# Attention with softmax normalised on GpSimd, every probability tile transposed by DMA, and V as the stationary operand

## The chip, the cores and the metric

The kernel runs on 1 core of one Trainium2 chip. Its time is the device time of one execution in microseconds (us). Before the change the median of three runs is 2014.84 us (2014.69 to 2027.13). A separate execution was profiled; its span, from the first to the last instruction, is 2008.4 us. The engines are PE (TensorE), DVE (VectorE), ACT (ScalarE), POOL (GpSimd) and SP (SyncE, which here only issues DMAs); PEld is the PE's weight load.

## What is computed

One transformer block with adaptive layer norm, on 2048 rows of width 640, batch 1:

```python
mod = silu(c) @ w_mod                       # six vectors of 640: sa, ca, ga, sb, cb, gb
h = layernorm(x) * (1 + ca) + sa
q = h @ wq                                  # 32 heads of 128; K and V come from a cache of 2048 rows
p = softmax(q @ k^T * 128**-0.5)            # 32 x 2048 x 2048
x = x + ga * ((p @ v) @ wo)
h = layernorm(x) * (1 + cb) + sb
u = gelu(layernorm(h) @ w1)                 # four column groups, shifted by +1, -1, +2, -2 rows
x1 = h + shifted(u) @ w2
x = x + gb * (x1 + gelu(layernorm(x1) @ w3) @ w4)   # width 1728 between w3 and w4
```

## The kernel before, in words

It is written by hand, engine by engine: each stage is a block with one instruction stream per engine, semaphores (`Ev`, `W`) order the streams, and a barrier ends the block.

**Head (L72-L176).** The six modulation vectors, then for 16 tiles of 128 rows layer norm on DVE, a transpose on PE and an evacuation on ACT into `hT`. Only when all 16 are done does the attention block begin.

**Attention (L179-L436).** 512 steps `s`: 32 heads of 16 query tiles of 128 rows. In a step PE multiplies a query tile with the 2048 keys (four matmuls of 512 columns into `Sps`, L327, two halves of 1024); DVE scales each half into `negS` and takes its minimum (L371); POOL takes the smaller of the two minima (L270); ACT makes the unnormalised exponentials `Pb` in bf16 (L399). Seven of eight tiles are transposed by a DMA from SP (L297), the eighth by PE (L312) with two copies by DVE (L363). Six steps later PE multiplies 16 transposed pieces as stationary operands with `Vaug` (V and a column of ones, 129 columns, L344), so that the row sum appears in column 128. DVE takes its reciprocal (L382), ACT scales the 128x128 result by it into `On` (L405), and POOL issues the DMA to DRAM (`o_scratch`, L285). For the next head PE transposes K and projects Q (`pe_job`, L228 and L233), ACT evacuates (L241, L244), and POOL issues all loads (L250-L256).

**Later stages.** Output projection with `wo`, residual and two layer norms per tile (L487, L525-L539), with `o_scratch` read back by DMA transposes (L471); a block for w1 and gelu (L585, L600); one for w2 and a layer norm (L618, L637); and one for w3, gelu, w4 and the end (L678-L714). Each begins with its own weight loads.

Of the kernel before, what the change touches and what calls it, by code (L numbers as in the profile page):

```python
# [8 lines left out]
F32 = mybir.dt.float32  # L9


class Ev:

    def __init__(self, nc, es, name):
        self.sem = es.enter_context(nc.semaphore(name))
        self.n = 0

    def inc(self, ins, k=1):
        ins.then_inc(self.sem, k)
        self.n += k  # L20
        return self.n


def W(eng, ev, val):
    if val > 0:
        eng.wait_ge(ev.sem, val)  # L26


def bass_adaLN_cond__mha_block_cached__mixer_s_mlp__prompt_kernel(
# [5 lines left out]
    assert DH == 128 and D % 128 == 0 and SQ % 512 == 0 and SK == 2048  # L35
# [5 lines left out]
    FL = FF - (NFT - 1) * 128  # L41
    G4 = D // 4
    SCALE = float(DH) ** -0.5
    EPS = 1e-5
    NG = H * NQT
    x2d = A_x[0]
    out2d = out[0]
    HD = D // 2
    NC2 = [(0, 512), (512, D - 512)]

    with ExitStack() as es:
        sb = lambda name, shape, dt: es.enter_context(nc.sbuf_tensor(name, shape, dt))
# [3 lines left out]
        mod_bc = sb("mod_bc", [128, 6 * D], F32)
        Sps = ps("Sps", [128, 2048], F32)
        PTp = ps("PTp", [128, 2048], BF16)
        Oaug = ps("Oaug", [128, 512], F32)
        QPp = ps("QPp", [128, 512], F32)  # L60
        QPb = QPp[:].bitcast(BF16)

        def ln_stats(v, src, st, mv, ev, ev2=None):
            v.bn_stats(st[:, 0:6], src[:, 0:HD])
            ev.inc(v.bn_stats(st[:, 6:12], src[:, HD:D]))
            W(v, ev, ev.n)
            (ev2 or ev).inc(v.bn_aggr(mv[:, 0:2], st[:, 0:12]))  # L67

        with ExitStack() as esA:
            sbA = lambda name, shape, dt: esA.enter_context(nc.sbuf_tensor(name, shape, dt))  # L70
            hT = sbA("hT", [128, KT, SQ], BF16)
            with ExitStack() as es0:  # L72
                sb0 = lambda name, shape, dt: es0.enter_context(nc.sbuf_tensor(name, shape, dt))
                c_sb = sb0("c_sb", [128, KT], BF16)
                c_f = sb0("c_f", [128, KT], F32)
                s_bc = sb0("s_bc", [128, KT, 128], BF16)
                ones_f = sb0("ones_f", [128, 128], F32)
                wmod = sb0("wmod", [128, KT, 6 * D], BF16)
                x_sb = sb0("x_sb", [128, NQT, D], BF16)
                st = sb0("st", [128, 2, 12], F32)  # L80
                mv = sb0("mv", [128, 2, 2], F32)
                sd = sb0("sd", [128, 2, 1], F32)
                rstd = sb0("rstd", [128, 2, 1], F32)
                xn = sb0("xn", [128, 2, D], F32)
                hA = sb0("hA", [128, 2, D], BF16)
                block = es0.enter_context(nc.Block())
                e_dc = Ev(nc, es0, "p_dc"); e_dw = Ev(nc, es0, "p_dw"); e_dx = Ev(nc, es0, "p_dx"); e_pool = Ev(nc, es0, "p_pool"); e_silu = Ev(nc, es0, "p_silu")
                e_sbc = Ev(nc, es0, "p_sbc"); e_mm = Ev(nc, es0, "p_mm"); e_mev = Ev(nc, es0, "p_mev")
                e_d = Ev(nc, es0, "p_d"); e_st = Ev(nc, es0, "p_st"); e_sq = Ev(nc, es0, "p_sq")
                e_hA = Ev(nc, es0, "p_hA"); e_tr = Ev(nc, es0, "p_tr"); e_hev = Ev(nc, es0, "p_hev")  # L90
                NCH = 8
                CW = 6 * D // NCH
                assert CW <= 512

                @block.sync
                def _(e):
                    with nc.allow_non_contiguous_dma(reason="tiny c vector"):
                        e_dc.inc(e.dma_start(c_sb[:], c[0].rearrange("(kt p) -> p kt", p=128)), 16)
                    e_dw.inc(e.dma_start(wmod[:], w_mod.rearrange("(kt p) n -> p kt n", p=128)), 16)
                    e_dx.inc(e.dma_start(x_sb[:], x2d.rearrange("(t p) d -> p t d", p=128)), 16)  # L100

                @block.gpsimd
                def _(g):
                    e_pool.inc(g.memset(ident[:], 0.0))
                    e_pool.inc(g.memset(ones_f[:], 1.0))
                    W(g, e_pool, 2)
                    e_pool.inc(g.affine_select(out=ident[:], in_=ident[:], pattern=[[-1, 128]],
                                               compare_op=ALU.not_equal, fill=1.0, base=0, channel_multiplier=1))

                @block.scalar  # L110
                def _(a):
                    W(a, e_dc, 16)
                    e_silu.inc(a.activation(c_f[:], c_sb[:], ACT.Silu))

                    def hev(qt):
                        b = qt % 2
                        W(a, e_tr, qt + 1)
                        e_hev.inc(a.copy(hT[:, :, qt * 128:(qt + 1) * 128],
                                         PTp[:, b * 1024:b * 1024 + KT * 128].rearrange("p (k q) -> p k q", k=KT)))
                    for qt in range(NQT):  # L120
                        b = qt % 2
                        W(a, e_st, qt + 1)
                        e_sq.inc(a.activation(sd[:, b], mv[:, b, 1:2], ACT.Sqrt, bias=float(EPS)))
                        if qt >= 1:
                            hev(qt - 1)
                    hev(NQT - 1)

                @block.tensor
                def _(t):
                    W(t, e_sbc, 1)  # L130
                    W(t, e_dw, 16)
                    for ch in range(NCH):
                        bank = Sps[:, (ch % 4) * 512:(ch % 4) * 512 + CW]
                        W(t, e_mev, ch - 3)
                        for kt in range(KT):
                            ins = t.matmul(bank, s_bc[:, kt, :], wmod[:, kt, ch * CW:(ch + 1) * CW],
                                           start=(kt == 0), stop=(kt == KT - 1))
                        e_mm.inc(ins)
                    W(t, e_pool, 3)
                    for qt in range(NQT):  # L140
                        b = qt % 2
                        W(t, e_hA, qt + 1)
                        W(t, e_hev, qt - 1)
                        for kt in range(KT):
                            ins = t.transpose(PTp[:, b * 1024 + kt * 128:b * 1024 + (kt + 1) * 128],
                                              hA[:, b, kt * 128:(kt + 1) * 128], ident[:])
                        e_tr.inc(ins)

                @block.vector
                def _(v):  # L150
                    W(v, e_silu, 1)
                    W(v, e_pool, 2)
                    for kt in range(KT):
                        ins = v.tensor_scalar(out=s_bc[:, kt, :], in0=ones_f[:], scalar1=c_f[:, kt:kt + 1],
                                              scalar2=None, op0=ALU.mult)
                    e_sbc.inc(ins)
                    for ch in range(NCH):
                        W(v, e_mm, ch + 1)
                        bank = Sps[:, (ch % 4) * 512:(ch % 4) * 512 + CW]
                        e_mev.inc(v.tensor_copy(mod_bc[:, ch * CW:(ch + 1) * CW], bank))  # L160
                    W(v, e_mev, NCH)
                    v.tensor_scalar_add(out=mod_bc[:, D:2 * D], in0=mod_bc[:, D:2 * D], scalar1=1.0)
                    e_d.inc(v.tensor_scalar_add(out=mod_bc[:, 4 * D:5 * D], in0=mod_bc[:, 4 * D:5 * D], scalar1=1.0))
                    W(v, e_d, e_d.n)
                    W(v, e_dx, 16)
                    for qt in range(NQT):
                        b = qt % 2
                        ln_stats(v, x_sb[:, qt, :], st[:, b], mv[:, b], e_d, e_st)
                        W(v, e_sq, qt + 1)
                        e_d.inc(v.reciprocal(rstd[:, b], sd[:, b]))  # L170
                        W(v, e_d, e_d.n)
                        e_d.inc(v.scalar_tensor_tensor(out=xn[:, b], in0=x_sb[:, qt, :], scalar=mv[:, b, 0:1],
                                                       in1=mod_bc[:, D:2 * D], op0=ALU.subtract, op1=ALU.mult))
# [5 lines left out]
            with ExitStack() as es1:  # L179
# [564 lines left out]
```

## Time and profile before

| what | us |
|---|---|
| median of three runs | 2014.84 |
| span of the profiled execution | 2008.4 |
| first attention op on DVE (L371) starts at | 104.1 |
| last one starts at | 1577.0 |
| first output-projection matmul (L487) starts at | 1624.8 |
| last one starts at | 1770.1 |
| PE, DVE, ACT, POOL busy | 1587.3, 1547.8, 1374.8, 662.8 |

The span falls into a head of 104 us, 512 attention steps in 1476 us, and 428 us behind them. Busy time is a union, and the PE's includes the latency of pipelined matmuls, so it doesn't say how near PE is to its peak. In the rows of the profile "x512 | 1025.2, 2003 | 213.9 <-POOL" reads: 512 instructions, busy 1025.2 us, 2003 ns one, and 213.9 us of idle time just before them that POOL ended most of. In a row of stretches stand the stretch and its length, busy time and count of PE, PEld, DVE, ACT and POOL, the granted PE clock (1.00 is full), the share of time in which DMA packets were under way (above 1 where packets overlap on an engine) and GB/s.

### The profile page before, as it was taken

What the parts mean: (1) busy time and instruction counts of PE and PEld (TensorE: products, weight loads), DVE (VectorE), ACT (ScalarE), POOL (GpSimd) and SP (SyncE); (2) the same over time, 40 slices, a digit from 0 to 9 for tenths busy, and PEclk for the clock granted to TensorE, in tenths of its full rate; (3) what the DMA queues carried; (4) which work ended last, traced back from release to release, by engine and by line L of the source; (5) the groups of instructions that cost most, each with busy time, mean ns of one, the idle gap of its engine ahead of it and who ended that gap; (6) DMA issues with size and microseconds to landing.
All of it is one profiled execution on the core that took longest, in us unless ns stands there. A gap on an engine that the chain in (4) does not pass through costs nothing. (4 is left out here: it accounts for less than half of the span.)

```text
span 2008.4 us, 39142 instructions
## 1 busy us (share of the span) xinstructions
PE 1587.3 (79%) x14480; PEld 993.0 (49%) x14708; DVE 1547.8 (77%) x3151; ACT 1374.8 (68%) x1428; POOL 662.8 (33%) x1321
## 2 busy tenths in 40 slices
PE   2388888888888888888888888888888469966798
PEld 1145555555555555555555555555555335533344
DVE  5588888898889888888888888888988437737025
ACT  1288888888888888888888888888888401143430
POOL 0224444444444444444444444444443200010000
PEclk7589999999999999999999999999999879989899
DMA  4189999999999989999988989999999775510201
GB/s 150 38 160 201 198 198 199 201 198 195 199 202 204 190 197 199 198 201 199 194 188 191 187 200 196 203 199 196 195 202 196 174 199 122 106 33 1 89 14 40
DMA packets 1044381, 333.95 MB, mean 166 GB/s; under 512 B 1011744, under 2 KB 1024992, under 8 KB 1044192
## 3 DMA queue, kind: packets, MB, share of 16 engines
q1 hardware_dynamic: 1013472, 275.81, 68.3%
q0 software_dynamic: 30720, 55.63, 10.6%
q8 instruction: 118, 1.93, 0.4%
q14 instruction: 71, 0.58, 0.1%
HBM read 60.26 MB, written 19.40 MB: 40 GB/s over the span
## 5 line engine op out<-in xcount | busy, mean ns | idle before, releaser
L371 DVE TENSOR_SCALAR_CACHE_REDUCE negS<-Sps 128x1024 f32<-128x1024 f32 x1024 | 1207.7, 1217 | 168.6 <-PE Sps L327 163.7
L399 ACT ACTIVATE Pb<-negS,nm 128x2048 bf16<-128x2048 f32 x512 | 1025.2, 2003 | 213.9 <-POOL nm L270 194.8
L327 PE MATMUL Sps<-KTs,QT 128*128 128x512 bf16 x1889 | 549.8, 387 | 162.7 <-DVE negS L371 142.2
L270 POOL TENSOR_SCALAR nm<-nm 128x1 f32<-128x1 f32 x512 | 145.3, 284 | 840.9 <-DVE negS L371 840.9
L327 PEld LDWEIGHTS Sps<-KTs,QT 128*128 128x128 bf16 x2048 | 154.3, 98 | 402.8 <-DVE negS L371 320.6
L344 PEld LDWEIGHTS PTp<-Vaug,PTs 128*128 128x128 bf16 x4096 | 263.0, 99 | 66.4 <-issue 24.0
L285 POOL DMA_DIRECT2D o_scratch<-On x512 | 289.3, 565 | 4.5 <-ACT On L405 4.0
L344 PEld LDWEIGHTS Oaug<-Vaug,PTs 128*128 128x128 bf16 x4096 | 259.6, 98 | 59.9 <-issue 1.1
L344 PE MATMUL PTp<-Vaug,PTs 128*128 128x129 bf16 x4096 | 286.9, 223 | 1.5 <-ACT On L405 1.2
L344 PE MATMUL Oaug<-Vaug,PTs 128*128 128x129 bf16 x4096 | 281.4, 220 | 0.0
L487 PE MATMUL Sps<-wo,OTj 128*128 128x128 bf16 (+1 forms) x1008 | 140.9, 301 | 38.6 <-DMA OTj<-o_scratch 37.8
L233 PE MATMUL QPp<-hT,wq 128*128 128x512 bf16 x607 | 155.9, 386 | 5.2 <-ACT QT L244 2.0
L487 PEld LDWEIGHTS Sps<-wo,OTj 128*128 128x128 bf16 x1024 | 80.1, 99 | 100.1 <-DMA OTj<-o_scratch 37.6
L435 ACT ACTIVATE sdB<-mvB 128x1 f32<-128x1 f32 x48 | 9.7, 203 | 158.3 <-DVE mvB L67 158.3
L312 PE MATMUL PTp<-ident,Pb 128*128 128x128 bf16 x1024 | 78.7, 220 | 43.3 <-ACT Pb L399 43.3
L256 POOL DMA_DIRECT2D Vaug<-in_A_v_cache_dram x128 | 104.9, 820 | 5.6 <-issue 5.5
L363 DVE COPY PTs<-PTp 128x1024 bf16<-128x1024 bf16 x128 | 86.8, 678 | 25.4 <-PE PTp L312 25.3
L250 POOL DMA_DIRECT2D Knat<-in_A_k_cache_dram x128 | 104.7, 820 | 0.4 <-issue 0.4
L709 DVE TENSOR_TENSOR t<-Sps,xb 128x640 f32<-128x640 f32 x16 | 13.2, 825 | 103.6 <-PE Sps L690 103.6
L405 ACT ACTIVATE On<-Oaug,rl 128x128 bf16<-128x128 f32 x256 | 89.7, 350 | 2.5 <-DVE rl L382 2.5
L405 ACT ACTIVATE On<-PTp,rl 128x128 bf16<-128x128 f32 x256 | 89.5, 350 | 2.0 <-DVE rl L382 2.0
L312 PEld LDWEIGHTS PTp<-ident,Pb 128*128 128x128 bf16 x1024 | 60.1, 98 | 54.6 <-ACT Pb L399 54.5
(72 smaller groups left out, 1127.6 us busy)
## 6 DMA issues: line engine op xcount, KB each, us to landing
Knat<-in_A_k_cache_dram POOLq DMA_DIRECT2D x128, 128.0 KB, 3.7
Vaug<-in_A_v_cache_dram POOLq DMA_DIRECT2D x128, 128.0 KB, 3.8
o_scratch<-On POOLq DMA_DIRECT2D x512, 32.0 KB, 3.3
PTs<-Pb SPq DMA_TRANSPOSE x448, 4.8
wq<-in_A_wq_dram POOLq DMA_DIRECT2D x32, 160.0 KB, 4.7
wo<-in_A_wo_dram SPq DMA_DIRECT2D x1, 5120.0 KB, 17.0
wmod<-in_w_mod_dram SPq DMA_DIRECT2D x1, 4800.0 KB, 14.8
x_sb<-in_A_x_dram SPq DMA_DIRECT2D x1, 2560.0 KB, 21.3
```

Of the source, the lines that this page charges most:

```text
L233: ins = t.matmul(QPp[:, 0:512], wq[:, hb, kk, :], hT[:, kk, cc * 512:(cc + 1) * 512], start=(kk == 0), stop=(kk == KT - 1))
L250: e_k[hb][pc // 2].inc(e.dma_start(Knat[:, hb, pc * 4:(pc + 1) * 4, :], A_k_cache[0, h, pc * 512:(pc + 1) * 512, :].rearrange("(t p) d -> ...
L256: e_v[hb].inc(e.dma_start(Vaug[:, hb, q * 4:(q + 1) * 4, 0:128], A_v_cache[0, h, q * 512:(q + 1) * 512, :].rearrange("(t p) d -> p t d", p ...
L270: e_nm.inc(g.tensor_scalar(out=nm[:, r8:r8 + 1], in0=nm0[:, r8:r8 + 1], scalar1=nm1[:, r8:r8 + 1], scalar2=None, op0=ALU.min))
L285: e_od[g_ % 8].inc(g.dma_start(o_scr[jj, :, hh, :], On[:, g_ % 8, :]), 16)
L312: ins = t.transpose(PTp[:, q * 128:(q + 1) * 128], Pb[:, b4, kt * 128:(kt + 1) * 128], ident[:])
L327: ins = t.matmul(Sps[:, col:col + 512], QT[:, hb, j * 128:(j + 1) * 128], KTs[:, hb, col:col + 512], start=True, stop=True)
L344: ins = t.matmul(ob[:, 0:129], PTs[:, b4, kt, :], Vaug[:, hb, kt, 0:129], start=(kt == 0), stop=(kt == NKT - 1))
L371: ins = v.tensor_scalar(out=negS[:, b, half * 1024:(half + 1) * 1024], in0=Sps[:, half * 1024:(half + 1) * 1024], scalar1=-SCALE, scalar2= ...
L399: e_exp.inc(a.activation(Pb[:, b4, :], negS[:, b, :], ACT.Exp, bias=nm[:, r8:r8 + 1], scale=-1.0))
L405: e_nrm.inc(a.activation(On[:, r8, :], OB[g_ % NOB][:, 0:128], ACT.Copy, scale=rl[:, r8:r8 + 1]))
L487: ins = t.matmul(YB[b][:, c0:c0 + cw], OTj[:, jj % 3, hh, :], wo[:, hh, c0:c0 + cw], start=(hh == 0), stop=(hh == H - 1))
```

## The change

Semaphores by hand are replaced by a list of operations (`Program.op`) with the tokens that each reads and writes: waits follow from the tokens, each engine runs its operations in the order in which they are written, and a DMA on SP waits in SP's queue for its inputs. An operation waits by a semaphore also for what its own engine wrote before it, where it reads that.

In the attention K arrives by DMA transpose (`ld_kt`). DVE's second half takes the first half's minimum as a per-row scalar, so no POOL operation joins them. ACT writes the exponentials in float32 (`E_`, 3 buffers) and their row sum by its accumulator; DVE takes its reciprocal two steps later; POOL multiplies the tile of 128x2048 by it into bf16 (`Pn`, 3 buffers); SP transposes every tile by DMA. Four tiles make a chunk (`PTs`, 3 chunks). V's pieces are stationary, 512 transposed columns stream, and 16 matmuls give O^T for four tiles. They are issued four to a step, two behind each half's score matmuls, and begin 8 steps behind the chunk's first tile (`PVL = 8`). ACT evacuates the chunk, and SP stores it transposed into `o_scratch`.

```diff
-                            ins = v.tensor_scalar(
-                                out=negS[:, b, half * 1024:(half + 1) * 1024],
...
-                        e_exp.inc(a.activation(Pb[:, b4, :], negS[:, b, :], ACT.Exp, bias=nm[:, r8:r8 + 1], scale=-1.0))
...
+                op("vector", lambda v: v.tensor_scalar(out=o_, in0=i_, scalar1=-SCALE, scalar2=nm0[:, r8:r8 + 1], op0=ALU.mult,
+                                                       op1=ALU.min, accum_out=nm[:, r8:r8 + 1]),
...
+            op("scalar", lambda a: a.activation(E_[:, be, :], negS[:, b, :], ACT.Exp, bias=nm[:, r8:r8 + 1], scale=-1.0,
+                                                accum_out=ls[:, r8:r8 + 1]),
...
+            op("gpsimd", lambda g: g.tensor_scalar(out=Pn[:, bp, :], in0=E_[:, be, :], scalar1=rl[:, r8:r8 + 1], scalar2=1.0,
+                                                   op0=ALU.mult, op1=ALU.mult),
...
+            op("sync", lambda e: e.dma_start_transpose(PTs[:, bt, :, q * 128:(q + 1) * 128], Pn[:, bp, :]),
...
+                    ins = t.matmul(O_ps[:, bo, :], Vs[:, hb, k, :], PTs[:, bt, k, :], start=(k == 0), stop=(k == NKT - 1))
```

The order within a step `s` of the attention (`pc, pq = divmod(s - PVL, 4)`; `ld_kt`, `ld_v` and `ld_wq` stand ahead of it):

```python
for half in range(2):
    qk(s, half); pv(pc, [two of 16 pieces]); qjob_mm(h + 1, ...); mx(s, half)
    if half == 0: rc(s - 2)                  # reciprocal
ex(s)                                        # exponentials
if s < NQT: head0(s)                         # layer norm and Q of the first head's later chunks
if pq == 3: oe(pc); od(pc)                   # evacuate and store a chunk of O^T
nz(s - 2); tr(s - 2)                         # POOL, then the DMA transpose on SP
```

In the head only the first 512 rows are normalised (on ACT) before the attention begins; the statistics of all 16 tiles and the modulation rows (`modbc_tasks`) still are. The other three groups of 512 rows run in `head0`, in the first head's first 12 steps. `wo` is loaded during the attention.

Behind the attention one block holds everything. A tile's transposes of the normalised rows are put off (`late`) until `flush()`:

```python
def op_tile(j):  y = outproj_pe(j); flush(); late.append(outproj_post(j, y)); ...
def w2_tile(j):  y = w2_pe(j);      flush(); late.append(w2_post(j, y))
for cc in range(4):
    for i in range(4):
        op_tile(4 * cc + i)
        if cc >= 1 and i == 0: flush()
        if cc >= 1 and i == 1:
            for n in range(5): w1_job(cc - 1, n)
        if cc >= 2 and i >= 2:
            for j in W2_AT[(cc, i)]: w2_tile(j)      # 0,1  2,3  4  5
load w3, w4; w2_tile(6); w2_tile(7); flush(); w1_job(3, 0..4); w2_tile(8..15)
for cc in range(4): 14 x w3_job(cc, f); 4 x w4_pe, w4_post
```

`o_scratch` now holds O^T and is read back by plain DMAs. The gelu of w1 and w3 has two PSUM banks in place of four.

**SP's queue in the attention.** Before, it is one kind of instruction:

```order
L289 UNCONDITIONAL_BRANCH [waits barrier_Pool_Activation_PE_DVE_SP_release]
L297 DMA_TRANSPOSE PTs<-Pb 128x16x128 [waits a_exp] x7
L297 DMA_TRANSPOSE PTs<-Pb 128x16x128 [waits a_pv,a_exp] x441
L179 UNCONDITIONAL_BRANCH
L465 UNCONDITIONAL_BRANCH [waits barrier_Pool_Activation_PE_DVE_SP_release]
```

Now, in one head (L401 is `tr`, L420 `od`, L213 `ld_kt`, L218 `ld_v`, L223 `ld_wq`):

```order
L401 DMA_TRANSPOSE PTs<-Pn 128x16x128 [waits a_gpsimd] x2
L213 DMA_TRANSPOSE KTs<-in_A_k_cache_dram 128x1x2048
L401 DMA_TRANSPOSE PTs<-Pn 128x16x128 [waits a_gpsimd] x2
L223 DMA wq<-in_A_wq_dram 128x5x256
L420 DMA o_scratch<-ost 128x4x128 [waits a_scalar]
L401 DMA_TRANSPOSE PTs<-Pn 128x16x128 [waits a_gpsimd] x4
L420 DMA o_scratch<-ost 128x4x128 [waits a_scalar]
L401 DMA_TRANSPOSE PTs<-Pn 128x16x128 [waits a_gpsimd] x4
L218 DMA Vs<-in_A_v_cache_dram 128x16x128
```

Each store of O^T waits for ACT between two transposes, and the loads have moved from POOL to SP.

**PE in the attention.** Before, across the end of a step (L327 scores, L344 a tile times V; a_dt6 is the transposed tile, a_nrm is ACT):

```order
L327 MATMUL Sps<-KTs,QT 128x512 [waits a_ev]
L327 MATMUL Sps<-KTs,QT 128x512
L344 MATMUL PTp<-Vaug,PTs 128x129 [waits a_nrm,a_dt6]
L344 MATMUL PTp<-Vaug,PTs 128x129 x15
L327 MATMUL Sps<-KTs,QT 128x512 [waits a_ev]
L327 MATMUL Sps<-KTs,QT 128x512
```

Now, at a chunk's first step (L365 `qk`, L409 `pv`, L314 `qjob_mm`; a_d11 and the like are transposes):

```order
L365 MATMUL S_ps<-KTs,QT 128x512 [waits a_vector]
L365 MATMUL S_ps<-KTs,QT 128x512
L409 MATMUL O_ps<-PTs,Vs 128x512 [waits a_d13,a_d18,a_d11,a_d17]
L409 MATMUL O_ps<-PTs,Vs 128x512
L314 MATMUL M_ps<-hT,wq 128x512 [waits a_scalar]
L365 MATMUL S_ps<-KTs,QT 128x512 [waits a_vector]
L365 MATMUL S_ps<-KTs,QT 128x512
```

One wait for four transposes now stands between the two halves of a step's scores.

**PE in the output projection.** Before, every tile's 64 matmuls stand ahead of an earlier tile's transposes (L442):

```order
L487 MATMUL Sps<-wo,OTj 128x128 x32
L442 MATMUL QPp<-ident,nrmB 128x128 [waits b_n]
L442 MATMUL QPp<-ident,nrmB 128x128 x4
L487 MATMUL Sps<-wo,OTj 128x512 [waits b_yd,b_wo,b_oj0]
L487 MATMUL Sps<-wo,OTj 128x512 x31
```

Now, at the tiles with i = 0 and i = 1 (L544 the projection, L528 the transposes, L591 w1):

```order
L544 MATMUL S_ps<-wo,OT 128x320 x63
L528 MATMUL O_ps<-ident,nrm 128x128 [waits b_vector]
L528 MATMUL O_ps<-ident,nrm 128x128 x4
L528 MATMUL O_ps<-ident,nrm 128x128 [waits b_vector]
L528 MATMUL O_ps<-ident,nrm 128x128 x4
L544 MATMUL S_ps<-wo,OT 128x320 [waits b_d4]
L544 MATMUL S_ps<-wo,OT 128x320 x63
L591 MATMUL M_ps<-nT,w 128x512 [waits b_d6]
L591 MATMUL M_ps<-nT,w 128x512 x9
L591 MATMUL M_ps<-nT,w 128x512 [waits b_scalar]
```

Two groups of transposes now follow each other there, the second for the tile just projected, and the w1 matmuls wait for ACT from the third group on.

More of the change, by code (lines that the diff above doesn't have):

```diff
@@ L9, with __init__ @@
 F32 = mybir.dt.float32
[L12 to L26, printed above, removed]
+class Op:
+    __slots__ = ("eng", "fn", "idx", "waits", "inc", "clock", "dma")
+    def __init__(self, eng, fn, dma):
+        self.eng = eng
+        self.fn = fn
+        self.dma = dma
+        self.waits = []
+        self.inc = False
+        self.clock = None
+        self.idx = 0
@@ L34, in bass_adaLN_cond__mha_block_cached__mixer_s_mlp__prompt_kernel @@
     FF = B_w3.shape[1]
[L35 removed]
+    assert DH == 128 and D == 640 and SQ == 2048 and SK == 2048
     KT = D // 128
@@ L45, in bass_adaLN_cond__mha_block_cached__mixer_s_mlp__prompt_kernel @@
     NG = H * NQT
+    HD = D // 2
     x2d = A_x[0]
     out2d = out[0]
-    HD = D // 2
-    NC2 = [(0, 512), (512, D - 512)]
+    GELU = ACT.Gelu_apprx_tanh
     with ExitStack() as es:
@@ L53, in bass_adaLN_cond__mha_block_cached__mixer_s_mlp__prompt_kernel @@
         ps = lambda name, shape, dt: es.enter_context(nc.psum_tensor(name, shape, dt))
-        o_scr = nc.dram_tensor("o_scratch", [NQT, 128, H, DH], BF16)
+        o_scr = nc.dram_tensor("o_scratch", [NQT, 128, H, 128], BF16)
         ident = sb("ident", [128, 128], BF16)
[L56 to L61, printed above, removed]
```

1180 lines of the change are left out of this document (571 added, 609 removed).

## The prediction

> **What bounds the kernel now.** First the stretches of the span, to see where the time lies, then the groups of the attention, then its timeline at a place where nothing is late.
>
> ```profile
> 0.00:104.00 104.00, 33.00 (x158) 15.77 (x160) 54.33 (x111) 20.91 (x42) 11.79 (x22) 0.64 0.26 91
> 104.00:1580.00 1476.00, 1221.50 (x12092) 799.44 (x12280) 1305.05 (x2681) 1261.24 (x1204) 638.29 (x1291) 0.99 0.97 196
> 1580.00:1624.00 44.00, 5.94 (x96) 5.56 (x96) 2.26 (x8) 4.32 (x9) 4.02 (x8) 0.60 0.77 233
> 1624.00:1780.00 156.00, 145.81 (x1088) 84.10 (x1104) 104.81 (x208) 17.56 (x48) 0.47 (x1) 0.96 0.49 101
> 1780.00:1863.00 83.00, 51.80 (x334) 26.97 (x340) 41.78 (x96) 36.04 (x70) 8.18 (x1) 0.93 0.07 20
> 1863.00:2009.00 146.00, 129.21 (x714) 61.17 (x728) 39.59 (x48) 34.71 (x58) 0.00 (x0) 0.94 0.14 49
> ```
>
> The attention is 1476 us, 2.88 us for each of 512 steps. In it DVE is busy 88%, ACT 85%, PE 83%: no engine is full. DMA, at a share of 0.97, looks full.
>
> ```profile
> L371 DVE TENSOR_SCALAR_CACHE_REDUCE negS<-Sps 128x1024 f32<-128x1024 f32 x1024 | 1207.7, 1217 | 168.6 <-PE Sps L327 163.7
> L399 ACT ACTIVATE Pb<-negS,nm 128x2048 bf16<-128x2048 f32 x512 | 1025.2, 2003 | 213.9 <-POOL nm L270 194.8
> L405 ACT ACTIVATE On<-Oaug,rl 128x128 bf16<-128x128 f32 x256 | 89.7, 350 | 2.5 <-DVE rl L382 2.5
> L244 ACT CAST QT<-QPp 128x512 bf16<-128x512 f32 x128 | 73.4, 573 | 9.6 <-PE QPp L233 9.6
> ...
> 109.93 1.22 DVE L371 TENSOR_SCALAR_CACHE_REDUCE negS<-Sps 128x1024 f32<-128x1024 f32 x1
> 111.07 0.08 DVE L371 DVE_READ_ACCUMULATOR negS<-Sps 128x1 f32 x1
> 111.23 1.22 DVE L371 TENSOR_SCALAR_CACHE_REDUCE negS<-Sps 128x1024 f32<-128x1024 f32 x1
> 111.25 0.28 POOL L270 TENSOR_SCALAR nm<-nm 128x1 f32<-128x1 f32 x1 [2.08 <-DVE negS L371]
> 111.57 2.00 ACT L399 ACTIVATE Pb<-negS,nm 128x2048 bf16<-128x2048 f32 x1 [0.36 <-POOL nm L270]
> 112.39 0.08 DVE L371 DVE_READ_ACCUMULATOR negS<-Sps 128x1 f32 x1
> 112.53 0.60 PE L327 MATMUL Sps<-KTs,QT 128*128 128x512 bf16 x2 [0.26 <-DVE negS L371]
> ```
>
> A half holds DVE's slot for 1.14 to 1.16 us (109.93 to 111.07), and its minimum is out 1.22 us behind its start (111.07 + 0.08). So DVE alone would do a step in 2.4 us; with its other work it reaches about 2.6, and ACT too. The 0.28 us above that are waits of engines for each other.
>
> ```profile
> SPq L297 <- ACT Pb L399: 715.4, 385, 26.6
> ...
> 1.82 0.52 SPq L100 DMA_DIRECT2D x_sb<-in_A_x_dram  x1
> ...
> L297 SPq DMA_TRANSPOSE PTs<-Pb x448: 1553/1732/5219, 108.9 to 1579.9; - x150
> DMA to landing us min/median/max: 3.6/4.8/9.0
> ...
> 1208.00:1210.00 2.00, 1.95 (x13) 0.94 (x12) 1.19 (x4) 1.90 (x3) 0.82 (x2) 1.00 1.27 288
> ...
> 1790.40:1800.00 9.60, 9.55 (x45) 4.39 (x45) 0.00 (x0) 9.38 (x17) 0.00 (x0) 0.99 0.00 0
> ```
>
> SP idled 715 us for ACT, and at 1208 DMA moved 288 GB/s for 2 us at a share of 1.27. So the attention's 196 GB/s at 0.97 isn't DMA's end: a tile of 0.524 MB can pass in 1.82 us. DMA's price is its latency, 4.8 us from issue to landing. The last row is for PE: 45 matmuls of 512 columns in 9.60 us, 0.213 each.
>
> **The change: the attention's step.** DVE now reads the first half's minimum before the second half starts: 1.22 and a hand-over of 0.04, then 1.2 (1.16 and a little for the scalar from memory), so 2.46 us a step without its two copies. ACT loses 0.35 us of scaling per step and K's copies: 2.0, plus a read of its accumulator (no row; DVE's takes 0.08), plus two copies of 0.57 in four steps, 2.4. PE: four score, four V and 1.25 Q matmuls of 0.213, 2.0. SP: 1.73 for each tile, 0.11 for K, 0.52 for a store in four steps and two loads in sixteen, 2.05. DMA: 1.06 tiles and 0.08 MB of V, stores and weights, 0.64 MB, 2.2 at 288 GB/s. None is above 2.5.
>
> POOL has no such row: what does 128x2048 times a per-row scalar cost?
>
> ```profile
> L270 POOL TENSOR_SCALAR nm<-nm 128x1 f32<-128x1 f32 x512 | 145.3, 284 | 840.9 <-DVE negS L371 840.9
> L574 POOL MEMSET us<- 128x10260 bf16 x1 | 8.6, 8647 | 191.2 <-POOLq L451 191.2
> L107 POOL TENSOR_SCALAR_AFFINE_SELECT ident<-ident 128x128 bf16<-128x128 bf16 x1 | 0.3, 288 | 0.2 <-POOL ones_f L105 0.2
> ```
>
> A memset writes an element in 0.843 ns (8647 / 10260). If arithmetic ran at that pace, the tile would take 284 ns + 2048 x 0.843 = 2.0 us. The select of 128 elements took 288 ns; if all of that were paid by the element, 2.25 ns, the tile would take 4.6 us, and midway between the two 3.3. I take 2.0, since an operation on one element already costs 284 ns and the select's 288 leaves almost nothing for its elements. The Trainium skill speaks against the move: "GPSIMD Engine Reference", "Engine selection", sends elementwise work to VectorE, calls GpSimd half as fast for two inputs and roughly at line rate for one; its section 3.1 gives 4497 ns for a two-input add of 2048 float32. By line rate the sum stays as it is, by 4497 ns (an estimate from that page) the step would be 4.65 us and the time about 2930; no run here shows it yet.
>
> So with POOL at 2.0 no engine decides, and the chain does. In PE's queue the first V matmuls of a chunk wait for its last tile, and the second half of the scores stands behind them. Call R the moment when DVE has read the first minimum of the step in which the reciprocal for that last tile is made. Then, by the rows above: reciprocal 0.08, hand-over to POOL 0.10 (111.15 to 111.25), POOL 2.0, to SP 0.05, landing 4.8, to PE 0.05: R + 7.08. Two V matmuls and one Q matmul 0.64, scores 0.60, to DVE 0.05: R + 8.37. The second half and the next first half take 1.2 + 1.22. That is one chunk, so four steps take 10.8 us, 2.70 a step. Each microsecond of POOL, DMA or SP on a chunk's last tile costs a quarter there. The landing lies between 3.6 and 5.8 (the median and 1 us for K's transfer or a store in front), which makes 2.46 (DVE's own floor) to 2.95. I take **2.75**, 0.05 above the chain because ACT's copies sit in front of an exponential with only two `negS` buffers: 512 x 2.75 = **1408 us**.
>
> **Head.** Loads are 8.9 MB.
>
> ```profile
> x_sb<-in_A_x_dram SPq DMA_DIRECT2D x1, 2560.0 KB, 21.3
> ...
> 16.14 9.67 PE L136 MATMUL Sps<-wmod,s_bc 128*128 128x480 bf16 x40 [16.14 <-DMA wmod<-in_w_mod_dram]
> ...
> 93.94 2.31 PE L233 MATMUL QPp<-hT,wq 128*128 128x512 bf16 x5 [0.68 <-ACT QT L244]
> 1777.83 0.71 PE L442 MATMUL QPp<-ident,nrmB 128*128 128x128 bf16 x5 [7.18 <-DVE nrmB L539]
> ...
> 27.47 0.49 DVE L64 BATCH_NORM_STATS2 st<-x_sb 128x6 f32<-128x320 bf16 x1
> 28.63 0.20 ACT L123 ACTIVATE sd<-mv 128x1 f32<-128x1 f32 x1 [23.41 <-DVE mv L67]
> ```
>
> Before, all of w_mod was there at 16.1 and x at 23 (1.82 + 21.3); the third that the column vectors need and the first x should be there at 12. Fifty one-column matmuls (0.15 each: five transposes of a cold PE took 0.71) end at 20; statistics of four tiles (1.16 each, 27.47 to 28.63) at 25; four normalisations on ACT (640 elements between L405's 128 and L399's 2048, 0.8 each) at 28.5; five rounds of transposing and copying through one bank, about 2.4 each, at 40.5; Q at 43.5; five rounds for the modulation rows of 2.31 + 0.57, which stand in PE's queue ahead of the first scores, at 58; **59 us** (45 to 75). Then `head0`: PE's transposes wait for ACT's copies, which stand behind that step's exponentials, so PE can't go on to the next step's scores. Such a step is scores 0.6, two halves 2.65, exponentials 2.1 and 0.95 for each further copy with its transposes: 7.3, 6.3 and 6.0 in place of 2.75; three groups of three, **33 us** (15 to 45).
>
> **Drain.** Behind the last minimum: exponentials 2.1, POOL 2.2, DMA 4.9, sixteen matmuls 3.4, copy 0.7, store 3.6 (the shortest landing), barrier and first read of 1 MB about 6: **23 us**, in place of 44, since `wo` is there.
>
> **Later stages.** The pace of a projection tile:
>
> ```profile
> 1707.39 0.44 PE L442 MATMUL QPp<-ident,nrmB 128*128 128x128 bf16 x5
> 1707.59 0.82 DVE L525 TENSOR_TENSOR tmpB<-Sps,mod_bc 128x640 f32<-128x640 f32 x1 [1.61 <-PE Sps L487]
> 1713.91 0.20 ACT L435 ACTIVATE sdB<-mvB 128x1 f32<-128x1 f32 x1 [3.23 <-DVE mvB L67]
> 1714.34 0.61 DVE L539 TENSOR_SCALAR nrmB<-xb,mvB,rstdB 128x640 bf16<-128x640 f32 x1
> 1716.36 0.44 PE L442 MATMUL Oaug<-ident,nrmB 128*128 128x128 bf16 x5
> ...
> 1834.88 0.82 DVE L637 TENSOR_TENSOR xb<-Sps,xb 128x640 f32<-128x640 f32 x1
> 1837.86 0.82 DVE L637 TENSOR_TENSOR xb<-Sps,xb 128x640 f32<-128x640 f32 x1
> ...
> 1787.00:1790.40 3.40, 2.98 (x7) 1.19 (x9) 0.00 (x0) 0.98 (x1) 1.18 (x1) 0.50 0.00 0
> ```
>
> 8.97 us a tile (1707.39 to 1716.36), set by PE; DVE's chain of 7.4 us (1707.59 to 1714.95) hides behind it. The change keeps PE's columns, so 16 tiles are 143.5. But `flush()` right behind a tile makes PE wait for that tile's whole chain. Three times at i = 0: 7.0 each, 21. w1 at i = 1: its gelu stands in ACT's queue behind this tile's second root, 6.5 us after the tile (1713.91 + 0.2), and two banks let PE do only two groups before; 12.5 us each, 37.5. Six w2 tiles 1.77 each, and a wait of 5.8 behind each of the four projections they follow, about 1.2 between two: 36. Together 238 until the last w2 tile of the loop. Then ten w2 tiles at DVE's pace of 2.98 (1834.88 to 1837.86) and w1's last group, 39. After an idle PE the granted clock is 0.50 for 3.4 us and 7 matmuls run where 16 would: eight such places at 2 us, 16. Sum **293 us**, in place of 239 (1624 to 1863). w3 and w4 are loaded behind other work, and the pace is PE's as before: **133 us** in place of 145, which began with the wait for w3.
>
> Sum: 59 + 33 + 1408 + 23 + 293 + 133 = 1949 us of span. The profiled execution lies 6.4 us below the median of the three runs (2014.84 - 2008.4), so I forecast **1956 us**. Without the attention's steps the sum is 541, so the span of before is reached at 2.87 us a step.
>
> **Rivals.** *POOL decides (slower).* If the tile costs POOL over 2.7 us, its own queue is longer than the chain, and from there on the change loses. At 3.3, with 0.15 of hand-overs, 541 + 512 x 3.45 + 6 = 2313 us. For it: nothing in the trace shows arithmetic at memset's pace. Against it: the select's 288 ns. 0.17. That is also what the rule of the Trainium skill's "GPSIMD Engine Reference" amounts to. *The engines wait for each other as before.* Before, 2.6 by the busiest engine became 2.88; the same 0.28 on top of the chain's 2.70 gives 2.98: 541 + 1526 + 6 = 2073. For it: buffers are fewer (two `negS`, three `Pn`), a store waits for ACT in SP's queue. Against it: the stall already gives each engine slack in a chunk. 0.16, a third of it so weak that the time stays. *Landing at its best.* At 3.6 the chain is below DVE's 2.46 and ACT's 2.4; 2.54 gives 541 + 1300 + 6 = 1847. For it: POOL's traffic leaves the rings. Against it: K and the stores join the transposes in SP's queue. 0.09. *The later stages do become one pipeline.* If the chains were covered at each flush, 293 would fall by the 21, 19, 26 and 16 of waits and cold clock: 1956 - 82 = 1874. For it: the DVE has work left over. Against it: PE's order, as shown. 0.07.
>
> **How the numbers follow.** The forecast has 0.51. Its own range, with landing, head and tail as bounded, is 1900 to 2025. The low end 1840 takes in the best landing, the high end 2150 takes in the mutual waits and POOL up to 3.1; about 0.2 is left out, mostly POOL at 3.3 and above. A measurement of this kernel can tell about 1% (the runs spread over 0.6%): below 1995 is faster, above 2035 slower. Faster: 0.40 of the forecast's 0.51, and 0.09 and 0.07. Slower: 0.17, 0.11 of the mutual waits and 0.02. The rest is the same.
>
> **What would show it.** POOL's mean of one near 2.0 us; DVE's first-half starts 2.7 to 2.8 us apart with a stall at every fourth step that ends with a transpose landing; the first minimum near 59 us; PE waits of 6 to 7 us on DVE in the projection; 133 us from the first w3 matmul. POOL above 2.7 us, or a DVE that never waits for PE, would prove the chain wrong.

## The result, and the profile after

The changed kernel takes 2233.99 us (median of four runs, 2230.11 to 2236.24), the kernel before 2014.76 us beside it: a ratio of 1.107, 95% interval 1.103 to 1.111. It is slower by a tenth; 1956 us with a range up to 2150 was forecast. The profiled execution has a span of 2228.0 us.

First the stretches of the changed kernel's span, cut at the terms of the sum: up to the first minimum, the first two heads (with `head0`), 29 undisturbed heads, the drain, the later stages up to w3, and the rest (the last head is left out).

```profile
0.00:57.60 57.60, 21.80 (x104) 9.33 (x105) 19.01 (x65) 14.52 (x23) 1.66 (x9) 0.85 0.55 164
57.60:212.00 154.40, 96.09 (x339) 38.81 (x337) 80.94 (x158) 93.91 (x106) 57.18 (x29) 0.78 0.68 142
212.00:1713.00 1501.00, 1149.22 (x4292) 407.24 (x4292) 1171.58 (x2321) 1080.83 (x1160) 914.46 (x464) 0.90 1.06 196
...
1763.00:1790.40 27.40, 11.48 (x32) 4.04 (x32) 0.16 (x1) 4.18 (x6) 4.98 (x5) 0.71 0.68 157
1790.40:2092.80 302.40, 220.86 (x1438) 143.17 (x1439) 142.80 (x299) 61.45 (x121) 0.00 (x0) 0.86 0.23 80
2092.80:2228.00 135.20, 126.55 (x738) 68.35 (x735) 41.92 (x54) 36.06 (x60) 0.00 (x0) 0.99 0.06 20
```

POOL's count in the third row is the number of steps: 464 in 1501 us, 3.235 us each, where 2.75 was forecast. Over 512 steps that is 248 us of the 279 by which the span of 2228 exceeds the sum of 1949. DVE, the busiest engine, is at 78% of them; DMA moves the same 196 GB/s as before. Next the groups of the attention, from the page.

```profile
L395 POOL TENSOR_SCALAR Pn<-E_,rl 128x2048 bf16<-128x2048 f32 x512 | 1009.1, 1972 | 757.8 <-DVE rl L391 498.8
L385 ACT ACTIVATE E_<-negS,nm 128x2048 f32<-128x2048 f32 x512 | 1025.0, 2002 | 481.3 <-DVE negS L379 468.8
L409 PE MATMUL O_ps<-PTs,Vs 128*128 128x512 bf16 x2048 | 681.7, 419 | 312.8 <-DMA PTs<-Pn 312.8
L379 DVE TENSOR_SCALAR_CACHE_REDUCE negS<-S_ps,nm 128x1024 f32<-128x1024 f32 x512 | 657.3, 1284 | 315.4 <-PE S_ps L365 295.0
...
L385 ACT ACTIVATION_READ_ACCUMULATOR E_<-negS,nm 128x1 f32 x512 | 95.5, 186 | 0.0
```

POOL, the feared engine, does its tile in 1.97 us. Read the last column as a chain: POOL waits for DVE, ACT for DVE, DVE for PE (295), and PE for a transpose's landing (313). One chunk shows it, in rows of SP, PE and DVE of the timeline:

```profile
913.65 0.36 SPq L420 DMA_DIRECT2D o_scratch<-ost  x1
914.06 10.01 SPq L401 DMA_TRANSPOSE PTs<-Pn  x4
...
922.34 0.16 DVE L391 RECIPROCAL rl<-ls 128x1 f32<-128x1 f32 x1
...
924.09 0.64 PE L409 MATMUL O_ps<-PTs,Vs 128*128 128x512 bf16 x2 [3.57 <-DMA PTs<-Pn]
...
926.05 1.28 DVE L379 TENSOR_SCALAR_CACHE_REDUCE negS<-S_ps,nm 128x1024 f32<-128x1024 f32 x1 [3.55 <-PE S_ps L365]
```

This is the stall that the prediction drew: it comes at the first step of a chunk alone (85 of these 116 steps take over 3.2 us, no other step does) and ends with a landing. Only it is 1.9 to 3.9 us long on average, by its place in the head, where the chain left about 1 (10.8 less four steps of 2.46). And four transposes keep SP busy for 10.01 us without a pause, 2.5 each, where 1.73 was taken. What that does to the chunk's last tile, the third of the four, is seen in POOL's row for it and in SP's:

```profile
914.96 1.97 POOL L395 TENSOR_SCALAR Pn<-E_,rl 128x2048 bf16<-128x2048 f32 x1 [0.59 <-DVE rl L391]
...
919.14 2.58 SPq L401 DMA_TRANSPOSE PTs<-Pn  x1
```

POOL is done at 916.93, and SP, still at the tiles in front, issues at 919.14: 2.2 us where the chain had 0.05 (1.1 us on average over the last tiles of the 29 heads). 4.95 us later PE goes on. The source view of L401 shows all 512 transposes; the landing is as forecast:

```profile
L401 SPq DMA_TRANSPOSE PTs<-Pn x512: 1317/2340/7495, 75.9 to 1770.0; - x171
...
DMA to landing us min/median/max: 4.2/4.7/9.5
```

And SP waits in front of a store, 81 times, in the view of its waits:

```profile
SPq L420 <- ACT ost L415: 115.3, 81, 8.7
```

### The profile page after: what moved, and what is told of

The parts are those of the page before. It is cut to its first block, busy times and chain, and to the rows that moved or that the text cites. A ratio compares the mean times of both kernels' runs of the same rounds, so it can differ in the third digit from the quotient of the medians.

```text
span 2228.0 us, 22469 instructions
## 1 busy us (share of the span) xinstructions
PE 1660.6 (75%) x7063; PEld 682.0 (31%) x7063; DVE 1497.2 (67%) x2977; ACT 1327.2 (60%) x1511; POOL 1010.9 (45%) x523
## 5 line engine op out<-in xcount | busy, mean ns | idle before, releaser
L395 POOL TENSOR_SCALAR Pn<-E_,rl 128x2048 bf16<-128x2048 f32 x512 | 1009.1, 1972 | 757.8 <-DVE rl L391 498.8
L385 ACT ACTIVATE E_<-negS,nm 128x2048 f32<-128x2048 f32 x512 | 1025.0, 2002 | 481.3 <-DVE negS L379 468.8
L409 PE MATMUL O_ps<-PTs,Vs 128*128 128x512 bf16 x2048 | 681.7, 419 | 312.8 <-DMA PTs<-Pn 312.8
L379 DVE TENSOR_SCALAR_CACHE_REDUCE negS<-S_ps,nm 128x1024 f32<-128x1024 f32 x512 | 657.3, 1284 | 315.4 <-PE S_ps L365 295.0
L365 PE MATMUL S_ps<-KTs,QT 128*128 128x512 bf16 x2048 | 675.3, 414 | 89.7 <-DVE negS L379 51.1
L375 DVE TENSOR_SCALAR_CACHE_REDUCE negS<-S_ps 128x1024 f32<-128x1024 f32 x512 | 624.8, 1220 | 96.0 <-PE S_ps L365 95.2
L409 PEld LDWEIGHTS O_ps<-PTs,Vs 128*128 128x128 bf16 x2048 | 205.1, 104 | 625.3 <-issue 441.8
L365 PEld LDWEIGHTS S_ps<-KTs,QT 128*128 128x128 bf16 x2048 | 176.0, 105 | 500.6 <-DVE negS L379 176.1
L314 PE MATMUL M_ps<-hT,wq 128*128 128x512 bf16 x640 | 278.5, 440 | 0.9 <-ACT hT L305 0.9
L544 PE MATMUL S_ps<-wo,OT 128*128 128x320 bf16 x1024 | 150.9, 311 | 8.6 <-DMA OT<-o_scratch 8.6
L544 PEld LDWEIGHTS S_ps<-wo,OT 128*128 128x128 bf16 x1024 | 103.6, 102 | 53.2 <-DMA OT<-o_scratch 9.1
L314 PEld LDWEIGHTS M_ps<-hT,wq 128*128 128x128 bf16 x640 | 71.2, 111 | 104.0 <-issue 43.3
L641 PE MATMUL S_ps<-wo,OT 128*128 128x320 bf16 x448 | 64.5, 300 | 2.8 <-ACT OT L631 2.8
```

What stands on the lines that cost most here:

```text
L314: ins = t.matmul(M_ps[:, 0, :], wq[:, wb, k, wo_:wo_ + 128], hT[:, k, cc * 512:(cc + 1) * 512], start=(k == 0), stop=(k == KT - 1))
L365: ins = t.matmul(S_ps[:, col:col + 512], QT[:, b, j * 128:(j + 1) * 128], KTs[:, b, col:col + 512], start=True, stop=True)
L375: op("vector", lambda v: v.tensor_scalar(out=o_, in0=i_, scalar1=-SCALE, scalar2=None, op0=ALU.mult, op1=ALU.min, accum_out=nm0[:, r8:r8 + ...
L379: op("vector", lambda v: v.tensor_scalar(out=o_, in0=i_, scalar1=-SCALE, scalar2=nm0[:, r8:r8 + 1], op0=ALU.mult, op1=ALU.min, accum_out=n ...
L385: op("scalar", lambda a: a.activation(E_[:, be, :], negS[:, b, :], ACT.Exp, bias=nm[:, r8:r8 + 1], scale=-1.0, accum_out=ls[:, r8:r8 + 1]) ...
L395: op("gpsimd", lambda g: g.tensor_scalar(out=Pn[:, bp, :], in0=E_[:, be, :], scalar1=rl[:, r8:r8 + 1], scalar2=1.0, op0=ALU.mult, op1=ALU. ...
```

## The experiments

Two readings of this were open. **Late** (called "SP's queue is late", and Theory B from the fifth run on): a store ahead of a transpose waits for ACT's copy, so a chunk's last tile is issued late; with less waiting the time comes back. **Rate** ("the transposes' data rate", later Theory A): the DMA queues are full at about 206 GB/s, and no order of waits helps. A smaller rival was the ring of three `Pn` buffers. The ratios below are to the kernel before, run on the same chip; its medians were 2007.7 to 2010.8 us, against 2014.8 beside the change, so differences of some 6 us between versions are not read as effects.

**Store behind the transposes (e1).** `od` leaves its place ahead of `tr(s - 2)` and stands behind it, two steps later.

```diff
-                    od(pc)
...
+                if s % 4 == 1 and 0 <= (s - PVL) // 4 - (0 if (s - PVL) % 4 == 3 else 1) < NCH:
+                    od((s - PVL) // 4 - (0 if (s - PVL) % 4 == 3 else 1))
```

> The store of a finished chunk is put two steps later in SP's queue, behind the transpose of the chunk's last tile, so that no transpose stands behind a wait for ACT's copy. Theory (SP's queue is late): the 2.3 us that SP loses in front of the tile 4c+9 are gone, the last transpose of a chunk is issued when POOL is done; the stall at the first step of a chunk falls from 2.0-2.7 us to about 0.9, at a head's first step from 3.9 to about 2.7: 5 us a head, 2234 - 160 = about 2075 us. Rival (three Pn buffers: POOL waits for landings) and rival (the transposes' data rate): order in SP's queue changes nothing, 2210 to 2240 us.

2172.12 us, ratio 1.081 (1.078 to 1.085): 62 us less, not 160. The store's wait is a part of the loss, and by itself the smaller one.

**Lag 10 (e2).** `PVL = 10`.

> V matmuls begin 10 steps behind a chunk's first tile in place of 8; nothing else changes. Theory (SP's queue is late and the lag is too short for it): a chunk's last landing now has 5 us more, PE doesn't wait for it, the stall at every fourth step goes to under 0.3 us, a step takes 2.65 us and the time is 574 outside the steps + 512 x 2.65 + 6 = about 1940 us (1900 to 2000). Rival (three Pn buffers) and rival (data rate): POOL still waits for a landing in each chunk, the step stays above 3.0 us and the time above 2110 us.

2150.36 us, 1.071 (1.068 to 1.074): 84 us less, not 294. The stretch from the third head on, then the largest row of its waits view:

```profile
207.00:1637.00 1430.00, 1102.87 (x4292) 359.48 (x4291) 1191.27 (x2321) 1069.88 (x1160) 913.17 (x464) 0.97 1.12 206
```

```profile
POOL Pn L395 <- DMA PTs<-Pn: 411.6, 339, 8.5
```

3.08 us a step. The stall has not gone: it has moved from PE to POOL, which now waits for its buffers to be read. The DMAs move 206 GB/s at a share of 1.12.

**Four `Pn` buffers (e3)**, `NB_P = 4`.

> Four Pn buffers in place of three (the fourth shares its place with the rows of s of the head). Theory (SP's queue is late): POOL runs ahead of SP, but the transposes are issued no earlier; POOL's wait of 158 us for landings mostly goes, the time falls by 0 to 30 us, 2205 to 2234. Rival (three Pn buffers bind): the chunk's last tile is normalised about 2 us earlier and the time falls below 2130 us.

2233.06 us, 1.111 (1.109 to 1.114). At lag 8 the ring is no cause.

**K and V loaded for two heads only (e4)**, `h < 1` in place of `h + 1 < H` for `ld_kt` and `ld_v`.

> K and V are loaded for the first two heads only and used again by all others (so the values of 30 heads are left out, the work on them is not). Theory (SP's queue is late): only the chunks behind a K transpose or V load gain, the stall at a head's first step from 3.9 to 2.0 us and at its fifth step from 2.7 to 2.0: 2.6 us a head, about 80 us, 2150. Rival (data rate): K and V are 1.0 of 9.6 MB of a head, the step falls by a tenth, 3.23 to 2.9 us, about 2065 us. Rival (three Pn buffers): as the theory.

2157.99 us, 1.075 (1.072 to 1.077): 76 us less. This fitted Late. But its step is still 3.09 us (the third to the last head's first minimum, 1435 us for 464 steps), so K and V are not what holds it there, and lag 8's waits cost something whatever the rate: without K and V the bytes of a step would pass in 2.69 us at the rate that e5 measures below.

**The DMAs alone (e5).**

> The attention's arithmetic is left out; only its DMAs are left, in SP's order, from buffers that never change, so nothing waits for an engine. Heads 0-7: the 128 tile transposes alone. Heads 8-15: with K, V, the weights and a store per four tiles on SP. Heads 16-23: the same, but V, weights and stores on ACT's queue. Heads 24-31: tiles and stores on SP. Theory A (the queue itself sustains about 206 GB/s, the 0.63 MB of a step take 3.0 us and no order of waits helps): 2.4-2.6 us a tile alone, 2.9-3.1 with all the rest, and the same 2.9-3.1 with the rest on ACT if the rings are full, 2.5-2.7 if SP's issuing is. Theory B (late issues and waits, as I held so far; 288 GB/s are to be had): 1.8-1.9 us a tile alone, 2.1-2.3 with the rest.

Rows of heads 0-7, 8-15 and 24-31 in the stretches view; no engine works, only the last two columns count:

```profile
100.00:360.00 260.00, 0.00 (x0) 0.00 (x0) 0.00 (x0) 0.00 (x0) 0.00 (x0) 0.50 1.14 211
400.00:750.00 350.00, 0.00 (x0) 0.00 (x0) 0.00 (x0) 0.00 (x0) 0.00 (x0) 0.50 1.12 213
1140.00:1450.00 310.00, 0.00 (x0) 0.00 (x0) 0.00 (x0) 0.00 (x0) 0.00 (x0) 0.50 1.12 210
```

A tile's 0.524 MB take 2.48 us; with K, V, stores and weights 0.633 MB take 2.97 at 213 GB/s. So with no engine to wait for, the attention's DMAs need 2.97 us a step, and Late cannot be the main cause. (The part on ACT's queue told nothing: ACT had nothing to wait for and issued all of it far ahead.)

**Lag 10 with four buffers (e6), and with the plain DMAs on ACT's queue as well (e7)**, `op("scalar", ...)` for V, `wq` and the store.

> Lag 10 and four Pn buffers together. Theory A (data rate): the step stays at 3.0-3.1 us, 2120 to 2155 us, as with lag 10 alone. Theory B (late issues, and with lag 10 the ring of three Pn buffers behind them): with the ring longer POOL no longer waits, the step falls to 2.65 us and the time to 1940 us (1900 to 2000).

> As the run before, with V, the weights and the stores on ACT's queue; K and the tiles stay on SP. If SP's issuing is what fills (0.97 of the time in the run with lag 10): SP has 2.35 us of transposes and 0.17 of K a step, ACT 2.47 and the issues, so about 2.65 us a step and 1940 us. If the rings' data rate is: 3.0 us a step and 2120 us, as with everything on SP.

2153.09 us, 1.071 (1.068 to 1.073), and 2164.31 us, 1.076 (1.073 to 1.079). With more buffers some engine still waits for a landing, and a second queue brings nothing: what is full lies behind the queues, not in SP's issuing. The DMA engines, which the queues share, are the likeliest place (a share of 1.12 in e2); no run singles them out.

**Half of every tile (e8)**, `PTs[:, bt, 0:8, ...]` from `Pn[:, bp, 0:1024]`.

> As the change (lag 8, three Pn buffers), but only the first 1024 of a tile's 2048 columns are transposed; PE reads old values in place of the other half. It takes 0.26 of 0.63 MB off a step. Theory A (data rate): the rate is no limit any more and what is left is the chain as predicted, at most 2.70 us a step: 574 + 512 x 2.60 to 2.70 + 6 = 1910 to 1965 us. Theory B (SP waits 2.3 us for ACT's copy in front of the tile 4c+9, and SP's queue is late for that): the wait stays, half of the stall with it: 2.85 us a step, 2040 us.

1977.83 us, 0.984 (0.981 to 0.986). The stretch of 29 heads, and its transposes in the source view:

```profile
202.00:1480.00 1278.00, 1089.47 (x4289) 361.99 (x4287) 1167.65 (x2321) 1080.62 (x1161) 914.14 (x465) 0.97 0.72 135
```

```profile
L403 SPq DMA_TRANSPOSE PTs<-Pn x512: 1231/1267/5936, 75.8 to 1526.9; - x171
```

2.75 us a step with the store still waiting in its place (this version leaves the second half of every tile untransposed, so only its time counts). Between the two theories' numbers, nearer A: the stall is left at one step of sixteen, the chunk whose last tile follows K's transfer in SP's queue.

**Wide stores (e9)**, lag 10 and `o_scr` as `[NQC, 128, H, 512]`.

> Lag 10, and the scratch for O^T laid out so that a store writes 1024 bytes in a row in place of 256; the projection reads back 256 in a row in place of 8192. Theory A with a price by the packet: a store costs 0.08 us a step in place of 0.16, the step falls by 0.08 and the time by 40 us against lag 10 alone, to 2110 us. With a price by the byte: 2150 us, as before.

2152.23 us, 1.072 (1.068 to 1.075): nothing gained.

**Later stages (e10)**, `while len(late) > 1: late.pop(0)()` in place of `flush()` in `op_tile` and `w2_tile`, and no flush at `i == 0`.

> The attention as the change has it; in the later stages the norm's transposes are issued one tile later (flush down to one entry in place of to none) and the flush in the first tile of a group is left out. By the prediction's terms (21 of waits at i = 0, 19 behind w2 tiles, 26 of w1, 16 of cold clock) 40 to 82 us less: 2150 to 2195 us. If PE waits there for something else: above 2210 us.

2198.64 us, 1.094 (1.089 to 1.098): 35 us less, just below what was expected. PE's wait at L528 in the waits view, as the change has it and in this run:

```profile
PE O_ps L528 <- DVE nrm L521: 61.3, 17, 7.0
```

```profile
PE O_ps L528 <- DVE nrm L521: 29.7, 13, 8.3
```

**All of it, and fewer bytes (e11).** Lag 10, four `Pn` buffers, the wide stores and e10's later stages, and PE transposes the second half of every fourth tile into the free PSUM bank; DVE and ACT copy it in turn.

```diff
+                nk = 8 if q == 0 else 16
+                op("sync", lambda e: e.dma_start_transpose(PTs[:, bt, 0:nk, q * 128:(q + 1) * 128], Pn[:, bp, 0:nk * 128]),
...
+                    for k in range(8):
+                        ins = t.transpose(MB[:, k * 128:(k + 1) * 128], Pn[:, bp, (8 + k) * 128:(9 + k) * 128], ident[:])
```

> Lag 10, four Pn buffers, wide stores, the later stages of the run before, and half of every fourth tile transposed by PE through the free PSUM bank, copied by DVE and ACT in turn, so that SP's queue carries 7/8 of the tile bytes. Theory A: 0.459 + 0.033 + 0.033 + 0.010 MB at 211 GB/s and the stores at half price, 2.61 us a step for the DMAs; DVE 2.56 + 0.08, ACT 2.47 + 0.13. A step of 2.70 to 2.80 us: 574 - 60 + 512 x 2.75 + 6 = about 1930 us (1890 to 1970), faster than both kernels. Theory B (waits, not the rate): the step stays above 2.95 us and the time above 2030 us.

1967.54 us, ratio **0.980** (0.976 to 0.984), within A's range of 1890 to 1970. It is the one complete version below both kernels, 2% below the kernel before. Its stretch:

```profile
300.00:1480.00 1180.00, 1005.17 (x4696) 380.45 (x4790) 1110.29 (x2182) 1022.83 (x1117) 838.29 (x427) 0.99 1.11 205
```

2.76 us a step. The rate is still 205 GB/s: the gain comes from carrying an eighth less of the tiles. That is 0.065 MB a step, 0.31 us at 211 GB/s, and the step fell by 0.32 against lag 10 alone; the buffers and the wide stores had brought nothing (e6, e9), the later stages 35 us outside the steps.

**Sizes alone (e12).** 

> The attention's arithmetic is left out again, only SP's DMAs run, all on one queue. Heads 0-5 tiles alone, 6-11 with a store of 256-byte runs per four tiles, 12-17 with a store of 1024-byte runs, 18-23 with a V load of 256-byte runs per four tiles, 24-29 with a V load of 4096-byte runs. Price by the byte at 211 GB/s: 9.92, 10.54, 10.54, 12.4, 12.4 us per four tiles. Price by the packet: 9.92, 10.54, 10.2, 12.4, 11.2 us.

By the transposes' starts, four tiles took 9.95 us alone, 10.64 and 10.54 with a store (256- and 1024-byte runs), 12.14 and 11.71 with a V load (256- and 4096-byte runs). Runs of 4096 help a load from DRAM by a fifth of its price; the stores hardly.

**Kinds alone, and the layout of `PTs` (e13 to e15).** One cause of the rate was left that the change itself brings: a tile's pieces now lie 1024 bytes apart (theory C; A now means that any transpose has this rate). e14 and e15 alter

```diff
-            PTs = sa_("PTs", [128, NB_T, NKT, 512], BF16)
+            PTs = sa_("PTs", [128, NB_T, 4, NKT, 128], BF16)
```

> The attention's arithmetic is left out; SP issues 96 transfers of 0.524 MB of each of five kinds, with a wait between the kinds: SBUF to SBUF transposes into runs of 256 bytes that lie 1024 bytes apart (as the change), the same into one run of 4096 bytes per partition (as the kernel before), transposes of K from DRAM into one run, plain copies into runs of 256 bytes 1024 apart, plain copies into runs of 4096. C (destination): 2.48 us, 1.8-1.9, 1.8-2.0, 2.4, below 1.8. A (any transpose): 2.48, 2.48, 2.5, and the plain ones below 2.2.

> The change with one thing altered: PTs holds each tile of a chunk as one run of 4096 bytes, and PE reads its 512 streamed columns as four runs of 128. C: the DMAs take 2.2 us a step as the prediction had it, and the chain decides: 2.70 to 2.85 us a step with the stalls behind K, 574 + 512 x 2.75 + 6 = 1988 us (1960 to 2040). A: 2234 us (2215 to 2245).

> The same with lag 10. C: nothing waits for a landing, DVE's 2.56 us decide, 2.58 to 2.65 us a step, 574 + 512 x 2.62 + 6 = about 1920 us (1900 to 1950), faster than both kernels. A: 2150 us as with lag 10 alone.

2231.38 us, 1.113 (1.109 to 1.118), and 2150.68 us, 1.072 (1.068 to 1.075): no difference. The five kinds of e13 in their order:

```profile
60.00:290.00 230.00, 0.00 (x0) 0.00 (x0) 0.00 (x0) 0.00 (x0) 0.00 (x0) 0.50 1.14 211
310.00:530.00 220.00, 0.00 (x0) 0.00 (x0) 0.00 (x0) 0.00 (x0) 0.00 (x0) 0.50 1.14 211
550.00:755.00 205.00, 0.00 (x0) 0.00 (x0) 0.00 (x0) 0.00 (x0) 0.00 (x0) 0.50 1.16 232
770.00:990.00 220.00, 0.00 (x0) 0.00 (x0) 0.00 (x0) 0.00 (x0) 0.00 (x0) 0.50 0.96 214
1010.00:1115.00 105.00, 0.00 (x0) 0.00 (x0) 0.00 (x0) 0.00 (x0) 0.00 (x0) 0.50 1.02 406
```

The layout is refuted (first and second row). A was right on the transposes within SBUF, but not in expecting plain copies below 2.2 us, where C was right: a plain copy in runs of 256 bytes takes 2.45 us, as long as a transpose, and in runs of 4096 bytes it is nearly twice as fast. So small packets point to where the rate comes from; no run had transposes in larger packets, so for them this is inferred. On the page of the changed kernel nearly all packets are small:

```profile
DMA packets 1294598, 366.38 MB, mean 164 GB/s; under 512 B 1267024, under 2 KB 1290512, under 8 KB 1292432
```

## Why the prediction was wrong

**The step that failed** is the one that opened DMA's account: "So the attention's 196 GB/s at 0.97 isn't DMA's end: a tile of 0.524 MB can pass in 1.82 us", and from it "DMA: ... 0.64 MB, 2.2 at 288 GB/s. None is above 2.5". A rate seen for 2 us was made a sustained one. e5 measures 211 to 213 GB/s, so the DMAs need 2.97 us a step, more than the chain's 2.70 and every engine. So "DMA's price is its latency" falls too. The trace of before held the warning. The 2 us ahead of the burst, and the 20 us around both:

```profile
1206.00:1208.00 2.00, 1.46 (x19) 1.13 (x19) 2.00 (x6) 1.47 (x2) 0.84 (x2) 1.00 0.35 72
...
1200.00:1220.00 20.00, 16.80 (x165) 10.79 (x166) 17.68 (x37) 17.71 (x19) 7.37 (x16) 1.00 0.96 197
```

The changed kernel has such bursts too, though its stretch of 29 heads stays at 196 GB/s, so a burst alone shows no room:

```profile
961.00:963.00 2.00, 1.64 (x6) 0.42 (x6) 1.95 (x6) 2.00 (x2) 2.00 (x2) 1.00 1.28 288
```

Before, with PE's eighth tile, a step moved 0.565 MB in all (196 GB/s for 2.88 us). At 211 GB/s that is 2.68 us, an estimate, below the 2.88 that the step took; the change hands PE's share to the DMAs.

**What this explains.** With lag 10 the step is 3.08 us, 0.11 above the DMAs' 2.97. From 2.75 to 3.08 are 169 us of the 248. The other 79 are what lag 8 adds, as e2's 84 us shows; e1 took back 62 us by moving the store alone. The two parts don't add up independently: with lag 8 kept, taking K and V away left 3.09 us a step (e4), and lag 10 with all bytes 3.08 (e2), but lag 10 with an eighth of the tiles less gave 2.76 (e11). The rate acts twice, as the sum of bytes and, at lag 8, as the time that SP needs per tile ahead of a chunk's last one. The prediction had that store in its second rival, with its queue, but priced SP at 1.73 a tile; a transpose holds SP for 2.34 in the changed kernel (half a tile in e8, where DMA's share is 0.72: 1.27).

A part of what lag 8 adds may be PE's clock, which the prediction counted in the later stages and put at nothing in the attention. Two score matmuls took 0.60 us before the stall shown above and 1.06 behind it:

```profile
919.92 0.60 PE L365 MATMUL S_ps<-KTs,QT 128*128 128x512 bf16 x2
...
924.96 1.06 PE L365 MATMUL S_ps<-KTs,QT 128*128 128x512 bf16 x2
```

In the 3.4 us from 924.1 on, the granted clock was 0.56:

```profile
924.10:927.50 3.40, 3.40 (x9) 1.22 (x10) 1.29 (x2) 0.12 (x1) 1.97 (x1) 0.56 1.11 217
```

Over the 29 heads the same 4292 matmuls kept PE busy 1149 us at a mean clock of 0.90, with lag 10 1103 us at 0.97. How much of these 46 us delays a step, no run separates.

**The chain** was right in its place: the stall at a chunk's first step, the landing at its end, V's first matmuls ahead of the second half's scores. Its term "to SP 0.05" was not: it assumed that SP is free when POOL is done. At half the bytes the step is 2.75 us, the number forecast, but by another route, and that is luck: DVE's own step is 2.56 us in place of 2.46, most chunks have no stall, and one long stall a head, in the chunk whose last tile stands behind K, makes up the rest.

**POOL** at 1.97 us beside 2.0, so the dearest rival fell as argued. The Trainium skill's "GPSIMD Engine Reference", section "Engine selection", calls one-input work "roughly line-rate"; the 1.97 us for 2048 elements agree. The 4497 ns of section 3.1 in the same page of the Trainium skill are for two inputs and don't carry over. **ACT's** accumulator read costs 186 ns, not DVE's 83; it lay beside the stall.

**Head, drain, later stages.** First minimum at 57.6 us (59 forecast). `head0`: 154.4 us for 32 steps, 51 above 32 x 3.235 (33 forecast, up to 45; the 5 MB of `wo` are loaded in it, but what they cost was not separated; the prediction's own three groups add up to 34). Drain 27.4 (23). Later stages 302.4 (293) and 135.2 (133). Their total error is 31 us with the sign of the result, far inside the range. The rival "one pipeline" promised 82 us if PE's order were mended; e10 got 35.

**The rivals.** POOL's 2313 us was nearest by its number and wrong by its mechanism. None of them had the DMAs' rate, since the step above had ruled it out.

## What to carry to other kernels

Ask of a DMA that looks full what the same traffic does alone, over hundreds of microseconds and in packets of the same size; a 2 us burst is no rate. If an engine's small share of a transfer (here PE's eighth tile) can be taken away "because DMA has room", price the room first: bytes of the step over the sustained rate. A wait that goes away when one buffer or lag is enlarged and comes back at the next engine points to a rate, not to an order.

## What the runs showed of the hardware

- DMA transposes of 128x2048 bf16 within SBUF: 211 GB/s, whether the tile is written as one run or in pieces, from DRAM 232. A plain copy in 256-byte runs has the same rate, 214, in 4096-byte runs 406. The Trainium skill's "Advanced Engine Details and Errata", section "X-Bar Transpose (TRN2)", calls transposes as fast as regular DMAs and expects 350-400 GB/s: the first holds here against plain copies in 256-byte runs, the second does not (211). The Trainium skill's "DMA: Bandwidth & Descriptors", section "Why small descriptors are slow (HBM only)", exempts transfers within SBUF: here 214 against 406 says otherwise.
- SP's time for issuing a transpose is no constant: 1.27 us (half tiles, DMA share 0.72), 2.34 in the changed kernel, 2.5 where four follow each other.
- Behind PE's stall of 3.57 us the granted clock was 0.56 over the next 3.4 us, and matmuls took up to 1.8 times as long.
- What stays open: why 288 GB/s pass for 2 us, in both kernels. In e5, where nothing pauses the queue, the tiles alone never moved more than about 225 GB/s in 2 us. That a burst is what piled up in a pause is a guess; no run separated it.
